# Streamed weights in whole rows, each load held back until a given step of the projections

## The chip, the cores and the metric

The kernel runs on one core of a Trainium2 chip. The metric is the device time of one execution in microseconds. A core has five engines that run their own instruction streams side by side and meet through semaphores: TensorE (PE, matrix products; its weight loads are shown as PEld), VectorE (DVE), ScalarE (ACT), GpSimd (POOL) and SyncE (SP), which here does nothing but issue transfers. Transfers (DMAs) between the main memory (DRAM) and the on-chip memory are carried out by 16 DMA engines that all queues share. An engine issues its transfers in the order of its program: one that waits holds up all that stand behind it on that engine.

## The reference

Four layers are applied in the order A, B, A, B to `x` of 2048 rows of 640. Layer A is attention with a memory that is carried from segment to segment; layer B is linear attention. The change is in layer A alone:

```python
h = jnp.concatenate([mem, xs], axis=1)            # 8 memory rows + 32 rows of x
q = jnp.einsum('btd,dhe->bhte', h, Wq)            # 640 -> 32 heads of 192
k = jnp.einsum('btd,dhe->bhte', h, Wk)
v = jnp.einsum('btd,dhe->bhte', h, Wv)
scores = jnp.einsum('bhqe,bhke->bhqk', q, k) * scale
scores = jnp.where(mask[None, None], scores, -1000000000.0)
p = _softmax(scores, axis=-1)
o = jnp.einsum('bhqk,bhke->bhqe', p, v)
o = jnp.einsum('bhte,hed->btd', o, Wo)            # 32 heads of 192 -> 640
mem = o[:, :M, :].copy()                          # the next segment's memory
```

There are 64 such segments in each layer A, one after another, since each needs the memory rows that the one before has made.

## The kernel before, in words

The weights of layer A don't fit into the on-chip memory. The kernel cuts the 32 heads into four rounds of eight heads (`NR`, 1,536 columns each, `PW`), and the 640 input rows into five chunks of 128 (`KC`, index `b`). A piece (m, r, b) is one chunk of one round of one of the matrices Q, K and V: 128 partitions with 3,072 bytes each, 384 KB. Most pieces stay in the on-chip memory (`res` in `layer_A`). Nine do not: for each of Q, K and V three chunks (b = 2, 3, 4; `SLOTS`) have a slot (`slot`) that holds the piece of round 0 or that of round 3. The output weights Wo of rounds 1 and 2 stay as well (`wo_mid`), and those of rounds 0 and 3 share one place (`wo_end`), which is loaded in six pieces of 320 KB (k = 0 to 5, two blocks of 128 rows each; `load_wo`).

The segments walk through the rounds forwards and backwards in turn (`rounds`): 0, 1, 2, 3, then 3, 2, 1, 0. So the round that ends a segment also begins the next one, and each slot is refilled once in a segment: in the first round of the segment its old content is used for the last time, and in the last round its new content is used. The same holds of `wo_end`.

What a segment does is written out in `A_chain` in the order of issue; nothing reorders it. `project` does one projection of 32 rows (8 of memory and 24 of x) for one round in five steps, one a chunk; a step is four matmuls side by side (line 882). In this order:

- first round, n = 0: Q, K and V (steps 1 to 15). In these projections the chunks with slots come first, and right after such a step the loop calls `load_slot` (line 885), which refills the slot with the piece of the last round. So the three loads of Q follow steps 1 to 3, those of K steps 6 to 8, those of V steps 11 to 13. For Q a load is a whole row of 3,072 bytes a partition, for K and V there are two loads of half a row each (lines 606 to 608).
- loop over n = 0, 1, 2 (line 1035): Q of round n + 1, the products of attention for round n - 1, the scores of round n, K of round n + 1, the output product of round n - 1 (`wo_round`, line 958), V of round n + 1. These are steps 16 to 30 (n = 0), 31 to 45 (n = 1) and 46 to 55 (n = 2, whose V comes after the loop). In n = 1, right after the first output product, whose weights are in `wo_end`, all six pieces of the last round's Wo are loaded into the same place (line 1053); in the last segment of a layer a copy of round 3's Wo for layer B follows (line 1055).
- the end (lines 1061 to 1094): V of the last round (steps 56 to 60), the output products of the last two rounds, with a few matmuls that only keep PE busy (`keep_busy`), and the transposition of the sum's first eight rows into the next segment's input (line 1092), with which the next segment begins.

SP issues the loads of weights and nothing else in the chain. A load waits for the matmuls that still read its place, and, as the trace shows, for the load issued eight before it, whose semaphore it takes over. POOL issues the small transfers: for the last eight rows of each segment, which don't depend on the memory, K, Q and V are computed ahead of the chain (`A_pre`) and fetched here for each round (lines 853 and 865), and what attention yields for them is stored (line 951) and multiplied with Wo in layer B, after the chain.

Of the kernel before, what the change touches and what calls it, by code (L numbers as in the profile page):

```python
# [112 lines left out]
class Kernel:  # L113
# [456 lines left out]
    def layer_A(self, xn_dram, at_dram, li, x_raw=None):  # L570
        nc, tc = self.nc, self.tc
        KC, NSEG = self.KC, self.NSEG
        dram = self.dram
        NR = 4
        PW = 1536
# [3 lines left out]
        wview = self.wview  # L579
        wov = self.A_Wo.rearrange("h d m -> (h d) m").rearrange("(c p) m -> p c m", p=P)  # L580
        low = self.view(0, LATE)
        at = LATE
        res, slot = {}, {}
# [16 lines left out]
        assert at + 36 * 1280 == ARENA  # L600
        unread = set(res)

        def load_slot(m, r, b, whole=False):
            if holds.get((m, b)) != r:
                holds[m, b] = r
                w = PW if whole or m == "Q" else PW // 2
                for h in range(0, PW, w):
                    nc.sync.dma_start(out=slot[m, b][:, h:h + w], in_=wview[m][:, b, PW * r + h:PW * r + h + w])

        def load_matrix(m, r):  # L610
            for b in range(KC):
                if (m, r, b) in unread:
                    unread.remove((m, r, b))
                    nc.sync.dma_start(out=res[m, r, b], in_=wview[m][:, b, PW * r:PW * r + PW])
                elif (m, r, b) not in res:
                    load_slot(m, r, b, True)

        early = {(0, 5), (2, 4), (2, 5), (1, 0), (1, 1), (1, 2), (1, 3)}

        def load_wo(r, into=None, part=range(6)):  # L620
            t = into if into is not None else wo_end[:, :] if r in (0, 3) else wo_mid[:, 7680 * (r - 1):7680 * r]
            for k in part:
                tk = t[:, 1280 * k:1280 * k + 1280]
                if r in (0, 3):
                    self.last_load = nc.sync.dma_start(out=tk, in_=self.wo_rows[r // 3, :, 1280 * k:1280 * k + 1280])
                else:
                    nc.sync.dma_start(out=tk.rearrange("p (c m) -> p c m", m=640),
                                      in_=wov[:, 12 * r + 2 * k:12 * r + 2 * k + 2, :])

        def piece(m, r, b):  # L630
            assert (m, r, b) in res or holds[m, b] == r
# [179 lines left out]
    def A_chain(self, xn_dram, at_dram, li, load_slot, piece, load_wo, late_wo, wo_mid, wo_end, low):  # L811
        nc, tc, KC, NSEG = self.nc, self.tc, self.KC, self.NSEG
        scale = float(self.Dh) ** -0.5
        NR = 4
        with tc.tile_pool(name=f"A{li}_ch", reuse_waits="tile", bufs=1) as sp, \
# [47 lines left out]
            def extra_v(s, n):  # L863
                r = rounds(s)[n]
                nc.gpsimd.dma_start(out=Vs[n % 2][64:80, :], in_=self.vb_d[s, r].rearrange("g t f -> (g t) f"))  # L865

            def project(hT, ps, m, n, s, steps):
                order = rounds(s)
                r = order[n]
                ns = SLOTS[m]  # L870
                for i in steps:
                    b = (i + KC - ns) % KC if n == 0 else i
                    w = piece(m, r, b)
                    for g in range(4):
                        if m == "V":
                            hp = 2 * (g % 2) + g // 2
                            rhs = w[:, 384 * hp:384 * hp + 384]
                        else:
                            w3 = w[:, 32 * g:32 * g + 32]
                            rhs = ap3(w3, [list(w3.ap[0]), [P, 6], [768, 2], [1, 32]])  # L880
                        o = ps
                        nc.tensor.matmul(o[32 * g:32 * g + 32, 0:384], lhsT=hT[:, b, :], rhs=rhs, start=(i == 0),  # L882
                                         stop=(i == KC - 1), tile_position=(0, 32 * g), skip_group_check=True)
                    if n == 0 and b >= KC - ns:
                        load_slot(m, order[NR - 1], b)

            def values(hT, n, s, pv, steps):
                project(hT, pv, "V", n, s, steps)
# [115 lines left out]
            hx_transpose(hT, range(4))  # L1004
            load_rows(1)
            for s in range(NSEG):
                W = pop.tile([P, 512], F32, name="ps_w", tag="w")
                order = rounds(s)
                L = NR - 1
# [25 lines left out]
                for n in range(L):  # L1035
                    raw = q_or_k("Q", n + 1)
                    if n > 0:
                        OT, o = attend(Ep, n - 1)
                        tails_after(n - 1)
                    S, E = weigh(False)  # L1040
                    to_rows(raw, "Q")
                    if n > 0:
                        otb = keep_tail(o)
                    next_kq(s, n)
                    if n > 0:
                        store_tail(otb, s, order[n - 1])
                    to_rows(q_or_k("K", n + 1), "K")
                    sums(S, E)
                    normalise(S, E)
                    if n > 0:  # L1050
                        wo_round(W, order[n - 1], OT, n == 1, False)
                        if n == 1:
                            load_wo(order[L])
                            if s == NSEG - 1:
                                load_wo(3, low[:, 0:7680])
                    if n + 1 < L:
                        pv = v_banks()
                        project(hT, pv, "V", n + 1, s, range(KC))
                        v_rows(pv, n + 1)
                    Ep = E  # L1060
                S, E = weigh(True)
                pv = v_banks()
                project(hT, pv, "V", L, s, range(3))
# [98 lines left out]
```

## Time and profile before

| what | value |
|---|---|
| time, median of 11 runs | 3843.6 us (3833.43 to 3861.41) |
| the profiled execution, its own time | 3855.02 us |
| its span, from first to last instruction | 3853.2 us |
| mean granted clock of PE | 0.974 |
| PE busy | 3562.7 us, 92% |
| DVE, ACT, POOL busy | 60%, 54%, 43% |
| read from and written to DRAM | 855.97 MB and 72.09 MB |
| first chain's first and last projection (line 882) | from 213.0 us; the last segment starts at 1621.9 us |
| second chain | from 2131.8 us; last projection at 3538.9 us |
| loads of K, of V: halves | 768 and 768 of 192 KB |
| loads of Q, of Wo by rows | 430 of 384 KB, 792 of 320 KB |

The two chains take some 2800 us of the span; the rest is the work ahead of them and layer B. "Issue to landing" of a transfer is from the start of the issuing instruction to the last of the 16 increments of its semaphore, one from each DMA engine. In a line of the waits, "engine A line <- engine B line" says that A's instructions of that line sat idle until B's ended, with the total in us, how often, and the longest; "issue" stands for idle time in which no wait shows. In a line of the windows there follow on the stretch the sums of each engine's busy time with its number of instructions (PE, PEld, DVE, ACT, POOL), the granted clock of PE, the mean busy share of the 16 DMA engines, and GB/s. In a line of the timeline stand start and length in us, engine, line, operation, what is written and read, and in brackets the idle time before it and what ended it.

### The profile page before, as it was taken

How to read it: one execution, taken by the hardware profiler on the slowest of the kernel's cores; microseconds unless marked ns; L12 is line 12 of the kernel's file. 1: busy time of each engine (PE TensorE's matmuls, PEld its weight loads, DVE VectorE, ACT ScalarE, POOL GpSimd, SP SyncE). 2: the span in 40 equal slices, each digit the busy share in tenths (PEclk: the TensorE clock that was granted, in tenths of full speed). 3: DMA queues.
4: the chain of work that ended last, by engine and by line, in shares of the span. 5: the costliest groups of instructions: out<-in, count | busy, mean ns of one | idle time of the engine just before them, and what ended most of it. 6: DMA issues, size and time to landing. Idle time of an engine off the chain costs nothing. (4 is left out here: it accounts for less than half of the span.)

```text
span 3853.2 us, 167748 instructions
## 1 busy us (share of the span) xinstructions
PE 3562.7 (92%) x70296; PEld 2246.7 (58%) x70312; DVE 2327.8 (60%) x6038; ACT 2073.5 (54%) x5285; POOL 1670.9 (43%) x4367
## 2 busy tenths in 40 slices
PE   7889999999999999989889999999999999999898
PEld 5655555556666565645457565565666665665453
DVE  3546666666666666646643566666666666664465
ACT  2245565556565666535432465565556665665453
POOL 2434444445555454440152455454454544553300
PEclk9999999999999999989899999999999999999899
DMA  9787788778787887860367887887888888788200
GB/s 324 241 263 268 257 284 276 264 257 286 272 293 268 281 280 274 279 193 1 110 208 227 277 289 265 272 287 271 276 272 286 279 283 275 266 297 298 80 1 28
DMA packets 587906, 935.20 MB, mean 243 GB/s; under 512 B 147322, under 2 KB 402826, under 8 KB 587146
## 3 DMA queue, kind: packets, MB, share of 16 engines
q1 hardware_dynamic: 449194, 805.76, 60.4%
q0 software_dynamic: 68288, 88.95, 7.7%
q10 hardware_dynamic: 69664, 29.76, 3.0%
q8 instruction: 551, 9.03, 0.9%
q14 instruction: 209, 1.71, 0.1%
HBM read 855.97 MB, written 72.09 MB: 241 GB/s over the span
## 5 line engine op out<-in xcount | busy, mean ns | idle before, releaser
L882 PE MATMUL ps_qk<-arena,hT 128*32 128x384 bf16 x20480 | 1007.1, 329 | 24.3 <-DMA arena<-in_A_Wk_dram 6.9
L882 PEld LDWEIGHTS <-hT 128*32 128x32 bf16 x30720 | 743.7, 97 | 477.5 <-DVE hT L1092 58.2
L892 ACT ACTIVATE raw<-ps_qk 128x384 bf16<-128x384 f32 x1024 | 503.0, 491 | 445.2 <-PE ps_s L985 250.1
L958 PE MATMUL ps_w<-arena,OT 128*32 128x160 bf16 x24576 | 556.4, 235 | 75.9 <-issue 45.9
L958 PEld LDWEIGHTS <-OT 128*32 128x32 bf16 x24576 | 439.2, 97 | 197.3 <-issue 104.0
L865 POOL DMA_DIRECT2D Vp<-vb x512 | 259.4, 507 | 679.2 <-PE ps_o L932 473.1
L882 PE MATMUL ps_v<-arena,hT 128*32 128x384 bf16 x10240 | 538.5, 329 | 2.8 <-issue 2.5
L897 DVE STREAM_TRANSPOSE KT<-raw 128x384 bf16<-128x384 bf16 x512 | 296.1, 578 | 198.6 <-ACT raw L892 194.7
L900 DVE STREAM_TRANSPOSE QT<-raw 128x256 bf16<-128x256 bf16 x512 | 228.0, 445 | 271.8 <-ACT raw L892 243.5
L853 POOL DMA_DIRECT2D kqb<-kqb x512 | 290.9, 568 | 165.7 <-POOL KT L861 147.8
L913 DVE CAST Vp<-ps_v 64x384 bf16<-64x384 f32 x512 | 286.1, 559 | 107.2 <-ACT Vp L911 92.1
L951 POOL DMA_DIRECT2D otb<-otb x512 | 283.3, 553 | 142.7 <-DVE otb L947 103.9
L911 ACT ACTIVATE Vp<-ps_v 64x384 bf16<-64x384 f32 x512 | 246.3, 481 | 160.9 <-PE ps_v L882 124.5
L938 DVE CAST OT<-ps_o 128x192 bf16<-128x192 f32 x512 | 183.2, 358 | 224.3 <-PE ps_o L932 206.1
L932 PEld LDWEIGHTS <-Vp 80*128 80x128 bf16 x4096 | 182.4, 99 | 195.2 <-issue 133.1
L992 DVE TENSOR_TENSOR E<-E,ps_s 80x320 bf16<-80x320 bf16 x512 | 247.4, 483 | 73.6 <-ACT ps_s L991 68.8
L971 ACT ACTIVATE E<-ps_s 80x320 bf16<-80x320 f32 x512 | 221.9, 433 | 114.9 <-PE ps_s L924 102.1
L932 PE MATMUL ps_o<-E,Vp 80*128 80x80 bf16 x4096 | 234.5, 202 | 33.8 <-DMA Vp<-vb 6.1
L924 PE MATMUL ps_s<-QT,KT 128*80 128x80 bf16 (+1 forms) x3072 | 234.4, 213 | 19.8 <-DVE KT L897 11.2
L858 POOL COPY QT<-kqb 128x64 bf16<-128x64 bf16 x512 | 126.5, 247 | 287.2 <-PE ps_s L924 282.9
L937 ACT ACTIVATE OT<-ps_o 128x192 bf16<-128x192 f32 x512 | 167.8, 328 | 140.0 <-PE ps_o L932 139.9
L965 PE MATMUL ps_idle<-arena,ident 128*128 128x384 bf16 x1024 | 235.7, 332 | 5.6 <-issue 5.6
(147 smaller groups left out, 5342.2 us busy)
## 6 DMA issues: line engine op xcount, KB each, us to landing
arena<-wo_rows SPq DMA_DIRECT2D x792, 320.0 KB, 5.9
arena<-in_A_Wq_dram SPq DMA_DIRECT2D x430, 384.0 KB, 4.5
arena<-in_A_Wk_dram SPq DMA_DIRECT2D x768, 192.0 KB, 5.6
arena<-in_A_Wv_dram SPq DMA_DIRECT2D x768, 192.0 KB, 5.1
kqb<-arena ACTq DMA_DIRECT2D x16, 1536.0 KB, 8.8
kqb<-kqb POOLq DMA_DIRECT2D x512, 48.0 KB, 4.9
arena<-in_A_Wk_dram SPq DMA_DIRECT2D x46, 384.0 KB, 7.6
arena<-in_A_Wv_dram SPq DMA_DIRECT2D x46, 384.0 KB, 7.6
```

What stands on the lines that cost most here:

```text
L853: nc.gpsimd.dma_start(out=kqb[:], in_=self.kqb_d[s, :, r, :])
L865: nc.gpsimd.dma_start(out=Vs[n % 2][64:80, :], in_=self.vb_d[s, r].rearrange("g t f -> (g t) f"))
L882: nc.tensor.matmul(o[32 * g:32 * g + 32, 0:384], lhsT=hT[:, b, :], rhs=rhs, start=(i == 0), stop=(i == KC - 1), tile_position=(0, 32 * g), ...
L892: nc.scalar.activation(out=raw[:], in_=ps[:, 0:384], func=ACT.Copy)
L897: nc.vector.transpose(out=KT[:, :, 0:64], in_=raw[:, :].rearrange("p (c j) -> p c j", j=64))
L911: nc.scalar.activation(out=o, in_=i, func=ACT.Copy)
L913: nc.vector.tensor_copy(out=o, in_=i)
L932: nc.tensor.matmul(O[x][:, 80 * i:80 * i + 80], lhsT=Vs[n % 2][0:80, 448 * x + k:448 * x + k + 128], rhs=E[0:80, 160 * x + 80 * e:160 * x ...
L951: nc.gpsimd.dma_start(out=self.otb_d[s, :, 96 * r:96 * r + 96], in_=otb[:, :, :].rearrange("p c t -> p (c t)"))
L958: nc.tensor.matmul(W[32 * g:32 * g + 32, 0:160], lhsT=OT[:, c, q:q + 32], rhs=w[:, 640 * i + 160 * g:640 * i + 160 * g + 160], start=(firs ...
L965: nc.tensor.matmul(ps[:, 0:384], lhsT=self.ident[:, :], rhs=wo_mid[:, 0:384], start=True, stop=True, skip_group_check=True)
L992: nc.vector.tensor_tensor(out=E[0:80, 0:320], in0=E[0:80, 0:320], in1=rc, op=ALU.mult)
```

## The change

`load_slot` always loads a whole row, so K and V take three loads of 384 KB instead of six of 192 KB each. The loads of Q stay where they are. Those of K and V are no longer issued after the step that frees the slot: they are put into a list, `pending`, in the order K 2, 3, 4, V 2, 3, 4, and so are the pieces 1 to 5 of Wo; piece 0 is issued as before. Each step of the projections calls `step_done` with its last matmul. At the steps named in `gates` the oldest entry of the list is issued, with a wait for that matmul added. So K is issued at steps 16, 20 and 24, V at 28, 33 and 37, and Wo's pieces 1 to 5 at 41, 45, 48, 51 and 53. The extra load of round 3's Wo in a layer's last segment moves to after the loop.

```diff
--- before.py
+++ after.py
@@ -600,12 +600,10 @@
         assert at + 36 * 1280 == ARENA
         unread = set(res)
 
-        def load_slot(m, r, b, whole=False):
+        def load_slot(m, r, b):
             if holds.get((m, b)) != r:
                 holds[m, b] = r
-                w = PW if whole or m == "Q" else PW // 2
-                for h in range(0, PW, w):
-                    nc.sync.dma_start(out=slot[m, b][:, h:h + w], in_=wview[m][:, b, PW * r + h:PW * r + h + w])
+                return [nc.sync.dma_start(out=slot[m, b], in_=wview[m][:, b, PW * r:PW * r + PW])]
 
         def load_matrix(m, r):
             for b in range(KC):
@@ -613,19 +611,22 @@
                     unread.remove((m, r, b))
                     nc.sync.dma_start(out=res[m, r, b], in_=wview[m][:, b, PW * r:PW * r + PW])
                 elif (m, r, b) not in res:
-                    load_slot(m, r, b, True)
+                    load_slot(m, r, b)
 
         early = {(0, 5), (2, 4), (2, 5), (1, 0), (1, 1), (1, 2), (1, 3)}
 
         def load_wo(r, into=None, part=range(6)):
             t = into if into is not None else wo_end[:, :] if r in (0, 3) else wo_mid[:, 7680 * (r - 1):7680 * r]
+            loads = []
             for k in part:
                 tk = t[:, 1280 * k:1280 * k + 1280]
                 if r in (0, 3):
                     self.last_load = nc.sync.dma_start(out=tk, in_=self.wo_rows[r // 3, :, 1280 * k:1280 * k + 1280])
+                    loads.append(self.last_load)
                 else:
                     nc.sync.dma_start(out=tk.rearrange("p (c m) -> p c m", m=640),
                                       in_=wov[:, 12 * r + 2 * k:12 * r + 2 * k + 2, :])
+            return loads
 
         def piece(m, r, b):
             assert (m, r, b) in res or holds[m, b] == r
@@ -864,6 +865,18 @@
                 r = rounds(s)[n]
                 nc.gpsimd.dma_start(out=Vs[n % 2][64:80, :], in_=self.vb_d[s, r].rearrange("g t f -> (g t) f"))
 
+            pending = []
+            gates = {16: 1, 20: 1, 24: 1, 28: 1, 33: 1, 37: 1, 41: 1, 45: 1, 48: 1, 51: 1, 53: 1}
+
+            def step_done(ins):
+
+                self.step += 1
+                for _ in range(gates.get(self.step, 0)):
+                    if pending:
+                        for load in pending.pop(0)():
+                            tc.add_manual_dep(load.ins, ins.ins.name,
+                                              mybir.DependencyInfo(mybir.DependencyClass.Sync, mybir.DependencyReason.DATA))
+
             def project(hT, ps, m, n, s, steps):
                 order = rounds(s)
                 r = order[n]
@@ -879,10 +892,14 @@
                             w3 = w[:, 32 * g:32 * g + 32]
                             rhs = ap3(w3, [list(w3.ap[0]), [P, 6], [768, 2], [1, 32]])
                         o = ps
-                        nc.tensor.matmul(o[32 * g:32 * g + 32, 0:384], lhsT=hT[:, b, :], rhs=rhs, start=(i == 0),
-                                         stop=(i == KC - 1), tile_position=(0, 32 * g), skip_group_check=True)
+                        ins = nc.tensor.matmul(o[32 * g:32 * g + 32, 0:384], lhsT=hT[:, b, :], rhs=rhs, start=(i == 0),
+                                               stop=(i == KC - 1), tile_position=(0, 32 * g), skip_group_check=True)
                     if n == 0 and b >= KC - ns:
-                        load_slot(m, order[NR - 1], b)
+                        if m == "Q":
+                            load_slot(m, order[NR - 1], b)
+                        else:
+                            pending.append(lambda m=m, r=order[NR - 1], b=b: load_slot(m, r, b))
+                    step_done(ins)
 
             def values(hT, n, s, pv, steps):
                 project(hT, pv, "V", n, s, steps)
@@ -1004,6 +1021,7 @@
             hx_transpose(hT, range(4))
             load_rows(1)
             for s in range(NSEG):
+                self.step = 0
                 W = pop.tile([P, 512], F32, name="ps_w", tag="w")
                 order = rounds(s)
                 L = NR - 1
@@ -1050,14 +1068,16 @@
                     if n > 0:
                         wo_round(W, order[n - 1], OT, n == 1, False)
                         if n == 1:
-                            load_wo(order[L])
-                            if s == NSEG - 1:
-                                load_wo(3, low[:, 0:7680])
+                            load_wo(order[L], part=range(1))
+                            pending += [lambda r=order[L], k=k: load_wo(r, part=[k]) for k in range(1, 6)]
                     if n + 1 < L:
                         pv = v_banks()
                         project(hT, pv, "V", n + 1, s, range(KC))
                         v_rows(pv, n + 1)
                     Ep = E
+                assert not pending
+                if s == NSEG - 1:
+                    load_wo(3, low[:, 0:7680])
                 S, E = weigh(True)
                 pv = v_banks()
                 project(hT, pv, "V", L, s, range(3))
```

## The prediction

> **What bounds the kernel now.** I read the page first, then the waits of PE, the windows and the timeline of one segment, and last the landing times of the streamed loads. PE is busy 92% of the span, but a busy PE is not the whole answer: the two long stretches are chains of 64 segments each, and the windows view of most of them shows the DMA engines at four fifths.
>
> ```profile
> 253.60:1621.90 1368.30, 1292.61 (x31220) 814.72 (x31212) 890.96 (x2418) 812.48 (x2166) 678.14 (x1857) 1.00 0.81 274
> 2161.60:3538.90 1377.30, 1315.13 (x31781) 830.86 (x31777) 906.96 (x2462) 831.23 (x2210) 690.85 (x1894) 0.99 0.82 279
> ```
>
> The last two columns are the DMA share and GB/s; the clock before them is full. PE leaves 76 and 62 us of the two stretches idle. One segment, from its first projection at 924.8 us, in windows:
>
> ```profile
> 924.80:926.30 1.50, 1.50 (x40) 1.00 (x44) 0.06 (x1) 1.39 (x5) 0.94 (x3) 1.00 0.27 54
> 926.30:930.30 4.00, 4.00 (x88) 2.34 (x84) 3.01 (x8) 2.26 (x6) 1.32 (x6) 1.00 0.97 343
> 930.30:934.30 4.00, 3.91 (x104) 2.56 (x100) 3.12 (x8) 2.97 (x10) 1.76 (x6) 1.00 0.98 316
> 934.30:938.30 4.00, 4.00 (x108) 2.58 (x96) 2.88 (x7) 2.51 (x8) 2.23 (x6) 1.00 1.08 374
> 938.30:942.30 4.00, 3.94 (x120) 2.64 (x123) 2.39 (x8) 2.75 (x7) 2.23 (x6) 1.00 0.99 368
> 942.30:944.30 2.00, 1.11 (x36) 0.62 (x26) 0.89 (x3) 0.48 (x1) 1.58 (x5) 1.00 0.34 120
> ```
>
> From 1.5 us after the segment's start the engines are full for 16 us without a break, then run dry. Who issues in that time, and what PE meets at its end, in the timelines of SP and of PE:
>
> ```profile
> 925.20 2.44 SPq L608 DMA_DIRECT2D arena<-in_A_Wq_dram  x3
> 927.73 2.77 SPq L608 DMA_DIRECT2D arena<-in_A_Wk_dram  x6
> 930.59 3.58 SPq L608 DMA_DIRECT2D arena<-in_A_Wv_dram  x6
> 934.48 3.66 SPq L625 DMA_DIRECT2D arena<-wo_rows  x6
> ...
> 947.69 0.33 SPq L608 DMA_DIRECT2D arena<-in_A_Wq_dram  x1
> ```
>
> ```profile
> 944.96 0.88 PE L958 MATMUL ps_w<-arena,OT 128*32 128x160 bf16 x40
> 946.30 0.32 PE L958 MATMUL ps_w<-arena,OT 128*32 128x160 bf16 x8 [0.47 <-DMA arena<-wo_rows]
> ```
>
> SP's loads follow one another until 13.3 us into the segment. The last wo piece, needed by the last eight matmuls of the last output round, lands late. So PE and the stream of weights are nearly balanced: a segment cannot be shorter than about 20.85 us (the shortest of the trace) and takes 22.2 us on average, the mean over the 126 segments that are followed by another; in the median the sixth wo piece lands 20.2 us after the segment's start, and an undisturbed PE wants it at 19.7. In the waits view:
>
> ```profile
> PE ps_w L958 <- issue: 45.9, 55, 2.0
> PE ps_w L958 <- DMA arena<-wo_rows: 28.4, 51, 2.3
> PE ps_qk L882 <- DMA arena<-in_A_Wk_dram: 6.9, 6, 2.3
> PE ps_o L932 <- DMA Vp<-vb: 6.1, 12, 1.0
> ```
>
> The output rounds wait 74.3 us in 106 waits, 0.70 us each, part of it put down to "issue". Over the segments, the last round alone takes 0.58 us more than its 0.78 us minimum on average, 75 us in 128 segments. That is the sum that this change can touch.
>
> **What the Trainium skill says.** "DMA: Bandwidth & Descriptors", section "Queues, rings and completion order": one copy is split over up to 16 engines' rings, which take turns between queues by the packet, and completion is the last engine's. The trace agrees: 16 increments a load, the last wo piece's first and last 2.3 us apart (medians 17.94 and 20.21). Same page, "Why small descriptors are slow (HBM only)": about 3 cycles a packet on top of one per 32 bytes; that makes two 1,536-byte packets 102 cycles and one of 3,072 bytes 99, an estimate of 3%. The trace's packet records say more: 65 ns typically for 1,536 bytes and 121 for 3,072, so 130 against 121, 7%. "Runtime: NRT & Kernel Launch", section "Instruction fetch mechanics": instructions arrive by DMA in 16 KiB blocks of 256, mostly hidden. The page has 551 packets on q8 for 140,608 PE and PEld instructions, 255 each, so the block is right; hidden is only partly right: the "issue" waits of PE in the loaded part of a segment end 1.2 to 1.6 us after such a packet ends.
>
> **The change, part by part.** Times are medians after the segment's start. Steps are the 60 groups of four L882 matmuls, 0.165 us apart within a projection.
>
> *Whole rows.* K and V go from 12 loads of 192 KB to 6 of 384 KB a segment, Q and wo stay. SP issues 15 instead of 21, at 0.33 to 0.42 us each; 6 x 0.4 = 2.4 us of SP that nobody waited for, since the engines are full behind it: nothing. On each engine a load is 8 rows, so 96 packets of 65 ns become 48 of 121 ns: 6.24 to 5.81 us, 0.43 us less, and six completion writes of 9 ns: 0.05. That is the upper end, 0.48 us. Lower end: nothing, because the landings of the middle engine are 1.08 and 1.17 us apart for Q's whole rows and 1.13 us for a pair of K's halves, and the summed packet time in the K stage exceeds the engines' time (share up to 1.03), so the packets overlap and something common seems to cap the rate. I take 0.2 us. No mechanism makes the larger packet slower here, so I exclude a loss from this part.
>
> *The six K and V loads held back.* First halves of K are issued at 2.0 us now, V's last at 9.3. Step n's matmuls start at 2.45, 3.10, 4.41, 5.44, 6.25 and 7.98 us for gates 16, 20, 24, 28, 33 and 37; with 0.33 us for the matmul and 0.1 for the semaphore the loads go out at 2.9, 3.5, 4.8, 5.9, 6.7 and 8.4. From issue to the first engine's landing is 2.6 us for the first Q load, of which 1.1 is its transfer, so data flow 1.5 us after issue: from 4.4, 5.0, 6.3, 7.4, 8.2 and 9.9. The quickest engine is done with Q at 5.2, and needs 1.1 us a row: 6.3, 7.4, 8.5, 9.6, 10.7. Each row is there before its predecessor is through, so no engine goes dry. Without that cover a microsecond of empty engines would be a microsecond on the last wo piece. Behind each waiting load on SP stand the later rows, the wo pieces and the next segment's Q loads; the readers are steps 53 to 55 (from 12.7 us) for K and 58 to 60 (from 15.6) for V. The last V row, 8.4 + 5.1 us to landing, lands at 13.5: 2 us to spare, so no new wait. Cost nothing.
>
> *The wo pieces.* Piece 0 still follows the first output round (issued at 10.0). Pieces 1 to 5 wait for steps 41, 45, 48, 51 and 53, which start at 9.8, 10.5, 11.0, 12.4 and 12.7: issued at about 10.6, 10.9, 11.4, 12.8 and 13.1, against 10.8 to 13.3 now. The quickest engine is busy with the piece before until 13.1, 14.1, 15.0, 16.1 and 17.0, the data are there from 12.1 to 14.6. Again nothing, either way.
>
> *Queue depth.* SP now has up to eight loads in flight (it waits for the eighth before), so eight halves or eight wo pieces. The gates make it shallower in the K and V stage, about 4 instead of 5.6 us to landing, which shortens what stands behind it, such as the small loads of POOL (5 us to landing there) and the instruction blocks. But PE's waits begin after 9 us, where the depth stays: 6 x 320 KB. I give 2 us of the 6.1 of Vp, bounds 0 and 40 (half of the roughly 90 us that PE loses to late instruction blocks and the like).
>
> *The rest.* The extra load_wo(3) of each last segment comes behind the same six pieces on SP as before: nothing. The gates put a wait on loads and a signal on matmuls; L882 matmuls carry such signals already and SP's wait instructions last 17 ns: nothing.
>
> *Sum.* If the last piece lands 0.2 us earlier, each of the 106 waits shrinks by that or by its length: at most 21 us, and 16 with the actual lengths of the last round in the segments. With 2 for Vp: 18 us. The profiled execution took 3855.0 us, span 3853.2 and 1.8 around it, so 3837; the median of the runs is 11.4 lower, 3843.6, and becomes 3826.
>
> **Rivals.**
> *It is hidden anyway.* The engines have a common cap and the whole rows save nothing; the gates reorder a queue that stays full. For it: the 1.13 us a row in both forms. Against it: 9 ns a packet. Time 3844, give or take 11.
> *Shallower queue pays.* The instruction blocks and small loads, not bytes, make the long waits (the 45.9 us of "issue"), and they come sooner everywhere. For it: POOL loads land in 2 us when the stream is dry and 5 when it is full. Against it: the depth does not change where PE waits. 40 to 100 us: about 3770.
> *The gates starve the end.* The place is the last wo piece, held to step 53. Its price: in the segments' lengths, landing 0.3 us later costs 38 us, 0.5 us later 64. It decides once the piece is issued later than the quickest engine's end of piece 4 less 1.5 us, that is after 15.5 us, or the V rows leave gaps of as much; my figure is 13.1. For it: a PE stall before step 53 now delays the load as well (its start is 13.3 at the ninetieth percentile). Against it: 2.4 us of margin. Time about 3885.
>
> **How the numbers follow.** Forecast 0.45 (gain 8 to 45, so 3799 to 3836), hidden 0.26, shallower queue 0.08, starved 0.21. One measurement here tells 0.3%, 11.5 us, from no change. Faster: 0.42 of the forecast and 0.08: 0.50. Same: 0.03 and 0.25: 0.28. Slower: 0.01 and 0.21: 0.22. The 80% range leaves out half of each outer case: 3778 to 3880; the forecast's own is 3799 to 3836.
>
> **What would show it.** Right: K and V loads 384 each of 384 KB, with about 4 us to landing; the waits of ps_w on wo_rows and issue together near 58 us; no waits of ps_qk or ps_v on K and V rows; the DMA share in windows as full between 1.5 and 17 us of a segment. Wrong: gaps in that share, wo pieces landing later than 20.2 us, or an "issue" sum that falls by more than half.

## The result, and the profile after

The changed kernel takes 3811.1 us in the median of 12 runs (3805.35 to 3830.04), against 3840.7 us of 47 runs of the kernel before: a ratio of 0.9927, 95% interval 0.9913 to 0.9941. The forecast was 3826 us. The profiled execution has a span of 3821.8 us, 31.4 us less than the 3853.2 of before.

The windows of the two chains, over nearly the same part of the segments as before:

```profile
251.20:1600.90 1349.70, 1285.92 (x31196) 813.74 (x31189) 890.40 (x2415) 811.17 (x2165) 678.13 (x1857) 1.00 0.79 278
2136.20:3507.10 1370.90, 1309.32 (x31777) 828.34 (x31773) 907.47 (x2462) 830.19 (x2209) 690.97 (x1894) 1.00 0.80 280
```

The stretches are 18.6 and 6.4 us shorter. PE idles in 125 us of them, not 138; the other half of these 25 us is PE's busy time, which I have not traced. The granted clock is 0.996 in the first stretch of both kernels and 0.993 before and 0.996 after in the second: by my estimate, if all of PE's 1,309 us there followed the clock, 3 us of the 25. The DMA share has fallen from 0.81 and 0.82 to 0.79 and 0.80 while GB/s have risen: the same bytes cost the engines less time. The waits of PE, in the output rounds and on the rows of K and of Vp:

```profile
PE ps_w L975 <- issue: 49.2, 60, 2.2
PE ps_w L975 <- DMA arena<-wo_rows: 9.0, 15, 1.5
PE ps_qk L895 <- DMA arena<-in_A_Wk_dram: 7.3, 6, 2.9
PE ps_o L949 <- DMA Vp<-vb: 0.4, 2, 0.2
```

The waits on wo pieces have shrunk from 28.4 to 9.0 us, those on Vp from 6.1 to 0.4; those put down to "issue" are as large as before (45.9). The K line is the same six waits as before (6.9 us), all in the first segment of each chain, so no new wait on a held row has come. The transfers on the page, and below them the halves on the page of before:

```profile
arena<-wo_rows SPq DMA_DIRECT2D x792, 320.0 KB, 5.9
arena<-in_A_Wk_dram SPq DMA_DIRECT2D x430, 384.0 KB, 5.3
arena<-in_A_Wq_dram SPq DMA_DIRECT2D x430, 384.0 KB, 4.6
arena<-in_A_Wv_dram SPq DMA_DIRECT2D x430, 384.0 KB, 5.8
```

```profile
arena<-in_A_Wk_dram SPq DMA_DIRECT2D x768, 192.0 KB, 5.6
arena<-in_A_Wv_dram SPq DMA_DIRECT2D x768, 192.0 KB, 5.1
```

The last number of a line is the time in us from issue to landing. K and V come in whole rows, K a little sooner after its issue than the halves did and V later. In one segment, from 945.3 us, windows, SP's timeline and PE's timeline show the new order and the wait that is left:

```profile
946.80:950.80 4.00, 4.00 (x88) 2.34 (x84) 3.01 (x8) 2.26 (x6) 1.32 (x6) 1.00 1.00 347
950.80:954.80 4.00, 3.91 (x104) 2.55 (x100) 3.13 (x8) 2.97 (x10) 1.75 (x6) 1.00 0.92 308
954.80:958.80 4.00, 3.21 (x89) 2.12 (x77) 2.89 (x7) 2.51 (x8) 2.22 (x6) 1.00 1.02 361
958.80:962.80 4.00, 3.34 (x87) 2.07 (x88) 1.29 (x4) 1.65 (x4) 1.37 (x3) 1.00 1.02 366
```

```profile
945.69 1.30 SPq L606 DMA_DIRECT2D arena<-in_A_Wq_dram  x3
948.12 2.30 SPq L606 DMA_DIRECT2D arena<-in_A_Wk_dram  x3
951.11 2.87 SPq L606 DMA_DIRECT2D arena<-in_A_Wv_dram  x3
954.65 5.98 SPq L624 DMA_DIRECT2D arena<-wo_rows  x6
```

```profile
957.68 0.34 PE L895 MATMUL ps_qk<-arena,hT 128*32 128x384 bf16 x2
959.46 0.99 PE L895 MATMUL ps_qk<-arena,hT 128*32 128x384 bf16 x18 [1.44 <-issue]
```

The DMA share of 0.92 in the second of these windows is no gap that the gates make: over all segments, each stretch of 2 us from 1.5 to 17.5 us has a mean share of 0.93 to 1.02, against 0.93 to 1.04 before.

PE stops after two of the twenty matmuls of one projection and goes on 1.44 us later. Nothing in the kernel separates the second from the third. What the trace has there is a packet of 16,384 bytes on the queue of instructions (q8), from 956.86 to 957.97 us: PE goes on 1.49 us after its end. I call such a stop a block wait. In all that follows it is counted as an excess of over 0.12 us, over what is usual at that place of a segment, in the gap between two matmuls of the chains that ends 1.1 to 1.7 us after a q8 packet has ended; the positions of the last output round, where a wo piece can be late, are counted apart as wo waits. The kernel before has 86.3 us of block waits (127) and 43.3 us of wo waits (80), the changed one 110.3 (165) and 7.0 (20). These sums are of one execution each, and another choice of what is usual moves them by some us (the smallest, of the kernel without K and V loads below, from 12.5 to 20).

That these are stops at the border between two blocks can be tested. The trace of before has 551 packets on q8 and 141,012 instructions of PE (matmuls, weight loads and 404 others), 256 to a packet. With PE's instructions numbered in this way, 84 to 98% of the block-wait time falls on the same 12 of every 256 numbers in thirteen of the fourteen profiles below; 5% of the chains' matmuls stand there, and 2 to 7% of the time of the other stops falls there, the wo waits apart. In the kernel without K and V loads it is 44%: about half of its small sum is not of this kind.

### The profile page after: what moved, and what is told of

It reads as the page before. It is cut to its first block, busy times and chain, and to the rows that moved or that the text cites. A ratio compares the mean times of both kernels' runs of the same rounds, so it can differ in the third digit from the quotient of the medians.

```text
span 3821.8 us, 166603 instructions
## 1 busy us (share of the span) xinstructions
PE 3542.2 (93%) x70296; PEld 2241.5 (59%) x70312; DVE 2329.7 (61%) x6038; ACT 2072.0 (54%) x5285; POOL 1670.9 (44%) x4367
## 5 line engine op out<-in xcount | busy, mean ns | idle before, releaser
L975 PE MATMUL ps_w<-arena,OT 128*32 128x160 bf16 x24576 | 548.0, 235 | 59.3 <-issue 49.2
```

The lines of the kernel that those rows point to most:

```text
L975: nc.tensor.matmul(W[32 * g:32 * g + 32, 0:160], lhsT=OT[:, c, q:q + 32], rhs=w[:, 640 * i + 160 * g:640 * i + 160 * g + 160], start=(firs ...
```

## The experiments

Each ratio is to runs of the kernel before that were timed together with that kernel. Two more numbers go with each kernel. One is when the last engine lands the last wo piece, in us after the segment's start (median). The other is how many bytes SP has under way on average from 6 to 19 us of a segment: each load counts from its issue, and a sixteenth of it leaves with each of its 16 increments.

| kernel | ratio to before, 95% | span | last wo piece | KB under way | block waits | wo waits | span less both |
|---|---|---|---|---|---|---|---|
| before | 1 | 3853.2 | 20.21 | 1133 | 86.3 | 43.3 | 3723.6 |
| after | 0.9927 (0.9913 to 0.9941) | 3821.8 | 19.71 | 1199 | 110.3 | 7.0 | 3704.5 |
| after, again | 0.9918 (0.9903 to 0.9934) | 3792.9 | 19.69 | 1185 | 78.2 | 5.3 | 3709.4 |
| rows, no gates | 1.0152 (1.0134 to 1.0170) | 3896.0 | 19.47 | 1366 | 195.3 | 0.4 | 3700.3 |
| gates, half rows | 1.0049 (1.0029 to 1.0068) | 3867.7 | 20.27 | 1157 | 94.5 | 45.6 | 3727.6 |
| no K and V loads | 0.9693 (0.9678 to 0.9708) | 3719.3 | 18.59 | 535 | 12.5 | 2.4 | 3704.4 |
| wo pieces not held | 1.0035 (1.0019 to 1.0051) | 3856.3 | 19.79 | 1299 | 129.1 | 6.5 | 3720.7 |
| all gates later | 1.0059 (1.0042 to 1.0076) | 3861.8 | 20.36 | 1254 | 125.1 | 32.1 | 3704.6 |
| wo in pairs | 0.9984 (0.9970 to 0.9998) | 3834.7 | 19.62 | 1308 | 119.6 | 9.9 | 3705.2 |
| last piece at step 60 | 0.9916 (0.9896 to 0.9936) | 3807.5 | 20.16 | 1100 | 67.5 | 38.8 | 3701.2 |
| last piece at step 56 | 0.9877 (0.9861 to 0.9894) | 3785.8 | 19.68 | 1122 | 57.3 | 9.2 | 3719.3 |
| last piece at step 58 | 0.9882 (0.9863 to 0.9901) | 3795.6 | 19.84 | 1128 | 61.3 | 13.7 | 3720.6 |
| last two at 55 and 57 | 0.9813 (0.9790 to 0.9835) | 3764.8 | 19.66 | 1108 | 46.2 | 8.7 | 3709.9 |
| last three at 51, 55, 57 | 0.9817 (0.9794 to 0.9840) | 3771.3 | 19.67 | 1072 | 44.3 | 7.5 | 3719.5 |

The last column is the test of the bookkeeping. The spans differ by 177 us; less the two kinds of waits they lie between 3700 and 3728. So these two waits hold most of what the kernels differ in, and the experiments ask what sets each. The time outside the chains alone varies by 13 us among the fourteen (998.5 to 1011.6), which is half of the spread of the last column.

**The changed kernel once more**, unedited, as a yardstick beside the next three.

> The changed kernel itself, as the yardstick of this group on the same chip. Every theory: ratio to the kernel before 0.991 to 0.995, as measured already.

The ratio repeats, 0.9918. Its block waits are 32 us fewer than in the first profile of the same kernel: that much one execution's sum can be off, and single readings of it below are read with this in mind.

**Whole rows without gates.** K and V rows are issued as soon as their slots are free, and the six wo pieces together:

```diff
-                        if m == "Q":
-                            load_slot(m, order[NR - 1], b)
-                        else:
-                            pending.append(lambda m=m, r=order[NR - 1], b=b: load_slot(m, r, b))
+                        load_slot(m, order[NR - 1], b)
...
-                            load_wo(order[L], part=range(1))
-                            pending += [lambda r=order[L], k=k: load_wo(r, part=[k]) for k in range(1, 6)]
+                            load_wo(order[L])
```

> K and V in whole rows, but every load issued where the kernel before issues it, and the six wo pieces together after the first output round. Theory R (whole rows shorten the stream, the gates do nothing): ratio 0.990 to 0.996, the last wo piece lands 0.4 to 0.6 us earlier in the segment than before. Theory G (the gates shorten what waits behind a deep queue, the rows do nothing): 0.998 to 1.003, landing as before. If rows need the gates, since eight whole rows in flight make the queue deeper: above 1.003.

3894.6 us, 1.5% slower than before. Its waits and its transfers:

```profile
PE ps_w L972 <- issue: 85.4, 91, 2.1
PE ps_v L895 <- issue: 11.0, 19, 1.2
PE ps_qk L895 <- issue: 9.9, 20, 1.0
PE ps_w L972 <- DMA arena<-wo_rows: 6.6, 8, 2.1
```

```profile
arena<-wo_rows SPq DMA_DIRECT2D x792, 320.0 KB, 6.6
arena<-in_A_Wk_dram SPq DMA_DIRECT2D x430, 384.0 KB, 6.5
arena<-in_A_Wq_dram SPq DMA_DIRECT2D x430, 384.0 KB, 4.5
arena<-in_A_Wv_dram SPq DMA_DIRECT2D x430, 384.0 KB, 8.4
```

The stream is the quickest of all with these loads: the last piece lands at 19.47 us, and wo waits are gone (0.4 us). But V takes 8.4 us to landing, "issue" waits in the output rounds go from 45.9 to 85.4 us and appear in the projections of Q, K and V too, and block waits more than double. SP may have eight loads in flight; eight whole rows are twice the bytes of eight halves, and 5.5 us into a segment 2,421 KB are under way, against 1,433 in the kernel before. So whole rows by themselves win at the end of the stream and lose more in PE's instructions, as the third of the forecasts had it. It is not the longer packet as such that does it: the changed kernel has the same packets and 110 and 78 us of block waits, not 195.

**Gates with half rows.** The schedule of the change, with `load_slot` giving two halves for K and V, both at their gate:

```diff
-        def load_slot(m, r, b):
+        def load_slot(m, r, b, whole=False):
...
-                return [nc.sync.dma_start(out=slot[m, b], in_=wview[m][:, b, PW * r:PW * r + PW])]
+                w = PW if whole or m == "Q" else PW // 2
+                return [nc.sync.dma_start(out=slot[m, b][:, h:h + w], in_=wview[m][:, b, PW * r + h:PW * r + h + w])
+                        for h in range(0, PW, w)]
...
-                    load_slot(m, r, b)
+                    load_slot(m, r, b, True)
```

> The gates of the changed kernel, but each K and V row still in two loads of half a row. Theory R: 0.998 to 1.003, the last wo piece lands where it did before, 20.2 us into the segment. Theory G: 0.990 to 0.996.

```profile
PE ps_w L977 <- issue: 49.5, 67, 1.8
PE ps_w L977 <- DMA arena<-wo_rows: 29.8, 56, 2.1
```

3855.3 us, 0.5% slower. Both waits stand where they stood before (45.9 and 28.4 us), and the last piece lands when it did, as the account in which the rows do all had it; the loss lies outside the ranges of both accounts and is not traced. The gates gain nothing here; that the queue is as shallow already, since eight halves bound it (1,157 and 1,133 KB), is the likely reason. Neither part of the change is faster alone; the gain is in the two together.

**No K and V loads in the chain.** The list gets an entry that only notes the slot's content, so the slots of K and V keep their first pieces: the loads are left out, and of the two rounds that share a slot one multiplies with the other's weights, which have the same size.

```diff
+            def keep_slot(m, r, b):
+                holds[m, b] = r
+                return []
...
-                            pending.append(lambda m=m, r=order[NR - 1], b=b: load_slot(m, r, b))
+                            pending.append(lambda m=m, r=order[NR - 1], b=b: keep_slot(m, r, b))
```

> The changed kernel without the six K and V loads of each segment (the slots keep the rows of the round that the preparation left there, so this part of the weights is wrong): 43% of the stream's bytes are gone. Its wo pieces then land by about 14 us, and no wait on them is left. Theory I (PE's waits without a visible cause are instruction blocks that arrive late behind a full queue): these waits go with the bytes, the issue sum of ps_w falls from 49 us to under 15, ratio 0.955 to 0.972. If those waits don't depend on the stream: issue sum 40 to 50 us, only the 9 us on wo_rows and the K waits go, ratio 0.985 to 0.992.

```profile
PE ps_w L979 <- DMA arena<-wo_rows: 8.9, 14, 1.6
PE ps_w L979 <- issue: 2.0, 7, 0.5
```

3718.6 us. The "issue" waits of the output rounds are all but gone, from 49.2 to 2.0 us, with nothing done to PE's instructions, to their blocks (551 packets on q8, as everywhere) or to the wo pieces. Half of the segments take no more than 20.85 us, the shortest of the trace of before. This shows that the "issue" waits come from the weights under way; that they are instructions that come late is what their place, at every 256th instruction and just after a q8 packet, says. Full DMA engines are not enough for it: from 11.5 to 15.5 us of a segment, while the wo pieces come, the engines' share is 0.95 to 0.96 here, against 0.99 to 1.00 in the changed kernel, but from 9 to 17 us some 850 KB are under way and not 1,350. The last piece was expected at about 14 us and lands at 18.59: it is still held to step 53. What K's and V's loads cost the changed kernel in all is 87 us (3805.2 of the same comparison less 3718.6).

**Only K and V held back.** The wo pieces are issued together, as in the kernel before:

```diff
-                            load_wo(order[L], part=range(1))
-                            pending += [lambda r=order[L], k=k: load_wo(r, part=[k]) for k in range(1, 6)]
+                            load_wo(order[L])
```

> The changed kernel with the gates on K and V alone; the six wo pieces follow the first output round together. Whole rows without any gate were 1.0152, the changed kernel 0.9918, and the difference seems to be instruction blocks that come late behind a deep queue (waits of about 195 against 80 to 110 us in the chains). If the depth counts where PE waits, after 9 us of the segment, the wo gates are the ones that matter: 1.003 to 1.013. If the K and V gates matter, because they keep the queue from filling up early: 0.990 to 0.997.

```profile
PE ps_w L975 <- issue: 67.9, 66, 2.7
PE ps_w L975 <- DMA arena<-wo_rows: 6.6, 12, 1.4
```

3858.1 us, 0.35% slower than before. The gates of the wo pieces are worth 1.1% (1.0035 to 0.9927), though without them the last piece lands only 0.1 us later (19.79) and wo waits are as small. What they change is what is under way, 1,299 KB against 1,199 and 1,185, and block waits, 129 us against 110 and 78. The rest of the difference of the profiles, 16 and 11 us, is in the last column.

**Everything later.** All gates 1 to 4 steps later:

```diff
-            gates = {16: 1, 20: 1, 24: 1, 28: 1, 33: 1, 37: 1, 41: 1, 45: 1, 48: 1, 51: 1, 53: 1}
+            gates = {20: 1, 23: 1, 27: 1, 32: 1, 35: 1, 38: 1, 45: 1, 49: 1, 51: 1, 54: 1, 55: 1}
```

> All gates one to four steps later: K and V at steps 20, 23, 27, 32, 35 and 38, wo at 45, 49, 51, 54 and 55, so that a load arrives about when the quickest engine has finished the one before. Theory D (depth delays the instruction blocks): ratio 0.983 to 0.990, waits for blocks down to 50 to 70 us, the last piece still lands at 19.7 to 19.9 us. Theory S (the gates starve the engines once they are later): the last piece lands at 20.2 us or later, ratio 0.993 to 1.002.

```profile
PE ps_w L975 <- issue: 61.7, 79, 2.4
PE ps_w L975 <- DMA arena<-wo_rows: 19.6, 48, 1.1
```

3866.1 us, 0.6% slower than before, and slower than either account had it. The DMA engines run dry once, from 5.5 to 7.5 us, where their mean share is 0.92 and not 0.99: the second K row lands on the middle engine at 8.24 us instead of 7.53, and the 0.6 to 0.9 us are not made up; the last piece lands at 20.36. Wo waits are 32 us again. This is the price of a gate that comes too late in the K and V stage. The queue, caught up later in the segment, is deeper there too (1,254 KB), so block waits don't fall.

**Wo in pairs.** Three loads of 640 KB at piece 0's place and at steps 45 and 51:

```diff
+        def load_wo_run(r, k0, k1):
+            ins = nc.sync.dma_start(out=wo_end[:, 1280 * k0:1280 * k1], in_=self.wo_rows[r // 3, :, 1280 * k0:1280 * k1])
+            return [ins]
...
-                            load_wo(order[L], part=range(1))
-                            pending += [lambda r=order[L], k=k: load_wo(r, part=[k]) for k in range(1, 6)]
+                            load_wo_run(order[L], 0, 2)
+                            pending += [lambda r=order[L], k=k: load_wo_run(r, k, k + 2) for k in (2, 4)]
```

> The changed kernel with the six wo pieces loaded in three of 640 KB (rows of 5,120 bytes), at once, at step 45 and at step 51. If larger packets shorten the stream as whole K and V rows did (9 ns a packet): 24 packets an engine fewer, 0.2 to 0.3 us earlier end; if nothing else changes, ratio 0.986 to 0.992. If the coarser loads make the queue deeper where PE fetches its instructions: 0.993 to 1.003.

```profile
PE ps_w L979 <- issue: 57.1, 61, 2.2
PE ps_w L979 <- DMA arena<-wo_rows: 8.2, 14, 1.5
```

3838.3 us, 0.2% faster than before, 0.6% slower than the change, as the second account had it. The packets of the chains' wo loads are 49,152 of 5,120 bytes in place of 98,304 of 2,560, and they save little: one takes 220.8 ns in the mean, two of the smaller 223.0 in the changed kernel, and the last piece lands 0.1 us earlier (19.62), not 0.2 to 0.3. Half of each pair is issued earlier than it need be, and 1,308 KB are under way.

**The last piece at step 60.** Step 53's gate goes to step 60 (issued at 16.96 us instead of 13.19). In this and the next kernels the extra load of a layer's last segment moves behind steps 59 and 60.

```diff
-            gates = {16: 1, 20: 1, 24: 1, 28: 1, 33: 1, 37: 1, 41: 1, 45: 1, 48: 1, 51: 1, 53: 1}
+            gates = {16: 1, 20: 1, 24: 1, 28: 1, 33: 1, 37: 1, 41: 1, 45: 1, 48: 1, 51: 1, 60: 1}
```

> The changed kernel with only the last wo piece held longer, to step 60 instead of 53, so issued at 17.0 instead of 13.2 us. By the prediction's third rival a piece issued after 15.5 us leaves the engines empty: 17.0 is 1.5 us past that for the quickest engine, and the slowest, which lands the last piece at 19.7, would hardly notice. Starved: last piece at 20.2 us or later, ratio 0.996 to 1.010. Not starved (the slowest engine, with its own backlog, sets the end): last piece at 19.6 to 19.9, ratio 0.985 to 0.993.

```profile
PE ps_w L975 <- DMA arena<-wo_rows: 30.1, 48, 2.6
PE ps_w L975 <- issue: 27.2, 35, 1.7
```

3810.1 us, as the change itself. Neither account holds as a whole: the landing is almost that of the starved one, the ratio that of the other. The piece is too late (20.16 us, 38.8 us of wo waits), but block waits fall to 67.5 us, and the two cancel. That a piece held far too long costs nothing on balance says that an earlier gate between the two should win.

**The last pieces as late as they are in time.** Three kernels measured together and a fourth after them. Each has one of the four new lines in place of the old, in the order in which they are told of:

```diff
-            gates = {16: 1, 20: 1, 24: 1, 28: 1, 33: 1, 37: 1, 41: 1, 45: 1, 48: 1, 51: 1, 53: 1}
+            gates = {16: 1, 20: 1, 24: 1, 28: 1, 33: 1, 37: 1, 41: 1, 45: 1, 48: 1, 51: 1, 56: 1}
+            gates = {16: 1, 20: 1, 24: 1, 28: 1, 33: 1, 37: 1, 41: 1, 45: 1, 48: 1, 51: 1, 58: 1}
+            gates = {16: 1, 20: 1, 24: 1, 28: 1, 33: 1, 37: 1, 41: 1, 45: 1, 48: 1, 55: 1, 57: 1}
+            gates = {16: 1, 20: 1, 24: 1, 28: 1, 33: 1, 37: 1, 41: 1, 45: 1, 51: 1, 55: 1, 57: 1}
```

> Only the last wo piece's gate moves, from step 53 to step 56, so it is issued about 15.7 us into a segment, not 13.2. The piece before it keeps the engines until about 17 us, so the last piece should land as before, within 0.2 us of 19.7. Theory that block waits follow the bytes SP has in flight: 1,199 KB falls to about 1,150, block waits from the 78 and 110 us of two profiles to about 75, waits on wo rows stay under 12 us; time 3795 to 3808 us, ratio 0.988 to 0.992. Theory that the gates work through the order of the transfers and not through their number in flight: as the changed kernel, ratio 0.991 to 0.994. Theory that it starves the end: 0.3 us later on the last landing, ratio 0.995 or more.

> The last wo piece waits for step 58, issued about 16.2 us into a segment. Bytes in flight: some 1,125 KB on average from 6 to 19 us; block waits about 70 us; the last piece lands 0.1 to 0.2 us later than in the changed kernel, so waits on wo rows 10 to 20 us. Theory of bytes in flight: ratio 0.988 to 0.992, between the changed kernel and the one held to step 56 or a little below both. Theory that order alone counts: 0.993 to 0.996, since only the late landing is left.

> The last two wo pieces wait for steps 55 and 57, issued about 13.7 and 15.9 us into a segment instead of 12.8 and 13.2. Theory of bytes in flight: about 1,110 KB on average from 6 to 19 us, block waits about 65 us, waits on wo rows under 15 us: ratio 0.987 to 0.991, the fastest of this call. Theory that order alone counts: as the changed kernel, 0.991 to 0.994. If the engines starve: last landing 0.3 us or more later, ratio 0.995 or more.

> The piece before those two moves as well, from step 48 to step 51 (issued about 12.8 us into a segment instead of 11.4); the engines reach it at about 14.6 us, so none should run dry. Theory of bytes in flight: 1,108 KB falls to some 1,090, block waits from 46 to about 40 us, waits on wo rows stay near 12 us: ratio 0.978 to 0.981. If the gain of the two pieces came from the last stage alone and is used up: 0.981 to 0.984. If an engine starves between the pieces, the last landing moves from 19.7 to 20.0 us or later: ratio 0.985 or more.

With one piece held to step 56 or 58: 3795.0 and 3795.6 us, 0.9877 and 0.9882. With two, to 55 and 57: 3772.2 us, 0.9813. With three: 3767.8 us, 0.9817, which is the same within the intervals. All four beat both kernels. The account in which only the order of transfers counts gave 0.991 or more for each of the first three and falls. That of bytes under way had the sign, and that two held pieces win most, but its sizes were short: it gave some 75, 70 and 65 us of block waits for the three, and there are 57, 61 and 46; and 0.987 to 0.991 for two pieces held. Waits and chain windows of the one with two pieces held:

```profile
PE ps_w L975 <- issue: 15.6, 28, 1.6
PE ps_w L975 <- DMA arena<-wo_rows: 11.8, 16, 1.7
```

```profile
252.30:1568.10 1315.80, 1275.47 (x31196) 808.35 (x31188) 890.51 (x2415) 809.72 (x2165) 675.58 (x1857) 1.00 0.82 285
2106.60:3448.90 1342.30, 1301.48 (x31773) 825.17 (x31769) 907.47 (x2462) 827.03 (x2209) 688.41 (x1894) 1.00 0.82 286
```

PE idles 81 us of the chains instead of 125, at 285 and 286 GB/s instead of 278 and 280. The last piece, issued 2.6 us later than in the changed kernel, lands at the same time (19.66 against 19.71). The third held piece takes off another 36 KB and adds nothing (44.3 against 46.2 us of block waits): the median, 0.9817, misses the 0.978 to 0.981 of the account of bytes under way and fits its rival, that the gain came from the last stage alone and is used up; but its interval, 0.9794 to 0.9840, reaches into both ranges, so this is not decided. By their start in the segment, the changed kernel has 71 of its 110 us of block waits from 17 to 20 us (some 49 in its second profile), the kernel with two pieces held 28 of 46; between 9 and 17 us the two have 39 (some 30) and 18. So the two held pieces bring less waiting in both stretches, most of it in the last.

## Why the prediction was right, and where it was not

**The direction and the wo waits: right.** The term that the forecast was built on, an earlier landing of the last piece, is what the change brings: wo waits fell from 43.3 to 7.0 us, and whole rows alone bring that (0.4 us) while gates alone don't (45.6). The gates came out at 2.8, 3.5, 4.8, 5.8, 6.6 and 8.4 us for K and V within 0.1 us of what was worked out, and at 10.2 to 13.2 us for pieces 1 to 5, within 0.4. No wait on a held row came of it.

**Whole rows, 0.2 us: mis-sized.** The last piece lands 0.50 us earlier on the last engine (20.21 to 19.71) and 0.65 on the middle one (18.70 to 18.05). That is the upper end, 0.48 us, or somewhat above. Worked out from mean packets, not typical ones: 96 packets of 70.5 ns are 6.77 us an engine and segment; those of K and V after, 48 of 131.2 (all 165,120 packets of 3,072 bytes at a mean of 136.0 ns, less the 66,816 that there were before at 143.1), are 6.30. With the six completions, 0.52 us. I had halved it because something common seemed to cap the rate. Nothing does at that rate: from 8 to 11 us of a segment the kernel before moves 369, 339 and 337 GB/s, that with whole rows alone 393, 397 and 402.

**"No mechanism makes the larger packet slower here, so I exclude a loss from this part": wrong.** Whole rows alone are 1.5% slower. Not the packet is slower for its bytes but eight of these loads hold twice the bytes, and the instruction blocks come later: block waits go from 86.3 to 195.3 us. The kernel before kept its queue shallow by the size of its loads, and I had not seen that the halves did this work.

**Queue depth: wrong.** I expected the gates to make the K and V stage shallower than before, with 4 us to landing, and to be worth 2 us. Landing took 5.3 and 5.8 us. From 7 to 10 us of a segment some 1,360 KB are under way, more than the 1,100 of before. The term itself, the waits on Vp, came out at 5.7 us (6.1 to 0.4) and not 2, but not by the gates: whole rows without gates have 0.4 us of these waits too, gates without whole rows 5.7. Against the kernel before the gates save nothing (0.5% slower by themselves); against whole rows without them they are worth 2.3% (1.0152 to 0.9918, measured together). They are the part that pays for the other, and I had costed the six K and V loads and the wo pieces at nothing because I compared each part with the kernel before and not with the kernel that has the other part.

**The sum: inside the range, in part by luck.** The medians are 29.6 us apart, and 18 us had been forecast: 16 of wo waits, 2 of Vp and nothing else. The wo waits fell by 36 and 38 us in the two profiles of the changed kernel, those on Vp by 5.7 and 5.6. So the term that carried the forecast has the right cause and less than half its size. What the forecast put at nothing, the instruction blocks, moved by 24 us up in one profile and 8 us down in the other; that it stayed so small is the meeting of two parts of which each alone is slower than before, and that was not foreseen.

The waits of ps_w came to 58.2 us, which I had put at 58; but the second profile of the same kernel has 38.0, so that agreement is luck. The 31 us by which the span fell are 36 fewer of wo waits, 24 more of block waits, and 19 fewer of neither; the 60 us of the second profile are 38 and 8 fewer, and 14 fewer of neither. Of these remainders, 5 and 4 us lie outside the chains (1004.8 us before, 1000.1 and 1000.9 after) and some 6 are the Vp waits; the rest I have not traced. What block waits gave or took in the changed kernel lies within what its two profiles differ by.

**The rivals.** "Hidden anyway" fell with the landing times. "Shallower queue pays" named the right mechanism, block waits that follow the queue, but this change does not make the queue shallower than it was. The kernel with the last two pieces held does so late in the segment (from 9 to 17 us some 1,180 KB are under way, against 1,310 before) and came out at 3772, close to the 3770 that this rival had; but of the 88 us by which its span is shorter, only 40 are block waits, 35 are wo waits. "The gates starve the end" did not happen, and its point of decision, 15.5 us, was too early: issued at 15.67 us the last piece lands when it did (19.68), at 15.99 it lands 0.13 us later (19.84), and only at 16.96 does it cost (20.16). I took the point from the quickest engine, which is through with the piece before at 16.6 us; the last piece's landing is set by the slowest, which is busy with it until 18.6 us.

## What to carry to other kernels

When loads are made larger, count the bytes in flight again and not only the packets: with a fixed number of loads in flight, a larger load is a deeper queue, and here PE's own instructions came later for it. A stop in the middle of a run of like matmuls, put down to "issue", ending some 1.4 us after a packet on the instruction queue and falling on the same place of every 256 instructions, is the sign. Then hold each load to the last moment at which its DMA engines are still busy with the one before; try the two halves of such a change apart, since each can lose and both together win.

## What the runs showed of the hardware

- Late instruction blocks cost 86 us of the kernel before, 195 with whole rows and no gates, and at most 12.5 without the K and V loads. The Trainium skill, "Runtime: NRT & Kernel Launch", section "Instruction fetch mechanics", calls the crossing of a block mostly hidden; here the measurement decides that it is hidden only while little else is under way. Over the twelve profiles with whole rows block waits rise with the KB under way, with small exceptions: 12.5 us at 535, 44 to 67 at 1,072 to 1,128, 78 and 110 at 1,185 and 1,199, 120 to 129 at 1,254 to 1,308, 195 at 1,366. The two with halves lie above that row, 86.3 at 1,133 and 94.5 at 1,157, so bytes alone are not the whole measure.
- The delay lies before the block's packet starts. In all fourteen profiles the counted stops end 1.41 to 1.45 us after the packet's end in the median (counted are those from 1.1 to 1.7), and the packet lasts about 1.0 us, whether the queue is deep or shallow. What grows is the time from PE's crossing of one border to the start of the next packet. In the chains exactly one packet starts between two crossings in 93 to 98% of cases (79% without the K and V loads). In these cases the slowest quarter starts more than 1.75 us after the crossing without the K and V loads, 2.35 with two pieces held, 2.70 before, 2.66 and 2.81 in the changed kernel's two profiles, and 3.38 with whole rows alone. That is the order of their block waits, and over all fourteen profiles it is so with small exceptions.
- What holds the packet back in that time is open: no record shows when the block was asked for. The same skill's "DMA: Bandwidth & Descriptors", section "Queues, rings and completion order", says that rings take turns by the packet, which there is a group of descriptors and not one row as in these records. That by itself would not lead one to expect that a deeper queue of equally large loads delays the block further.
- Two packets of 1,536 bytes take 141 ns in the mean, one of 3,072 takes 131. That is 7% of an engine's time for the same bytes. From 2,560 to 5,120 bytes it is 1% (223.0 and 220.8 ns).
